# Decode attention with a gated MLP on one core: a PV product with 32 weight columns and 512 moving columns, its diagonal summed on VectorE, and half of V29 queued ahead of K31

## The chip, the core and the metric

One NeuronCore of a Trainium2 chip runs the whole kernel. TensorE (PE) multiplies matrices out of the on-chip memory SBUF into the accumulators PSUM; a matmul is a weight load (its stationary operand) and a stream of moving columns. VectorE (DVE) and ScalarE (ACT) work element by element, SyncE (SP) issues the transfers, and sixteen DMA engines carry them out. Each engine works through its own instructions in order and waits at semaphores for the others. A DMA transfer is split over the sixteen DMA engines, and it has landed when all sixteen have finished their part.

The metric is the device time of one execution in microseconds (us), the median of some runs.

## What is computed

One decoding step for four sequences (B = 4, one token each, D = 640): attention over a sliding window of W = 2048 cached positions with H = 32 heads of Dh = 192, beside a gated MLP (F = 1536), both on the normalised input, added to it. The caches are bfloat16, and the kernel has to read 100 MB of K and as much of V.

```
xn = layernorm(x)
q = (xn @ wq) as [B, H, 1, Dh]
k, v = the last 2048 positions of k_cache, v_cache      # [B, H, 2048, Dh]
p = softmax(einsum("bhqd,bhkd->bhqk", q, k) * Dh ** -0.5)
o = einsum("bhqk,bhkd->bhqd", p, v)
attn = o as [B, 1, H * Dh] @ wo
mlp = (silu(xn @ w1) * (xn @ w3)) @ w2
out = x + attn + mlp
```

## The kernel before

**Layout.** One partition in 128 stands for one of 32 blocks of positions and one of the four sequences (P = 32 x 4); each block has NJ = 64 positions. A K or V tile of one head is 128 x 64 x 192 in bfloat16, 3 MB, and is one transfer. K has two buffers, V three. At the start the V buffers hold wq.

**One head.** The work of a head is cut into GQ = 4 quarters of 16 positions, called units (u = 4 h + quarter; NU = 128 in all):

- `mult` (L227, VectorE): product of a quarter of K with the head's q, 128 x 3072.
- `adder` (L238, TensorE): six matmuls with the identity as weights add groups of 32 of the 192 products in PSUM.
- `reduce_quarter` (L246, VectorE): sums the remaining 32, which gives the scores `sc`.
- `chain_lmax`, `chain_tr`, `chain_gmax`, `chain_bc`, `chain_z` (L250 to L282): maximum over all partitions of a sequence, exponential (`ex`), row sums (`rsum`), and `z`: the exponentials spread over four columns, of which only the own sequence's is not zero.
- `pv` (L290, TensorE): 32 matmuls per head, each with the weights of two positions (2 j x 4 b = 8 columns) against the 2 x 192 = 384 columns of V at these positions. Four strips of PSUM partitions (c = jj % 4, each 32 apart) are used in turn. In the result only the blocks where the position of the weight column and that of the moving column agree are wanted. ScalarE copies the bank to `o_sb` (L297).
- `ge_sum` (L315, TensorE, float32): two products with the selecting weights `sel_w`, one for each position of a pair, each over 192 columns read with a step of six, sum the wanted blocks into the head's 32 partitions of `po`. `ge_tot` (L302) puts the softmax's denominators into a last column of `po`.

**Groups of four heads.** `ge_rec` (L308) inverts the denominators, `ge_turn` scales (`og`, L320) and transposes in blocks of 32 (`oT`, L323), and `ge_proj` (L208) multiplies by the group's part of wo into the accumulator `acc`, which also takes the MLP's output (`ffn_out`) and x itself.

**The order.** The program is written out by hand: each piece of work is put into a numbered slot with a phase, and the slots are emitted in order, within one by phase and then by the order of adding. Slot u holds `mult` of unit u, `adder` and `reduce_quarter` of unit u - 1, and pieces of earlier heads. `pv` of head h is put L = 8 slots after the head's first unit, and `ge_sum` one slot later, except for the last three heads, which have slots of their own (`ends`, L373).

**The loads.** All but the first load (x) come from SyncE in the order of the slots. K of head h is issued at slot 4 (h - 1), when the last product on K of head h - 2 has freed its buffer; V of head h two slots after its first unit. The last three V loads are issued late: V29 at slot NU - 7 = 121, one slot after K31, then V30, V31 (in two halves), w2 in three parts, and the last two parts of wo. At the very end stand `ffn_out(0)`, `ge_proj` of the last two groups, and `ffn_out(1)` and `(2)`, then `res` (L437) and the two stores of the result.

Of the kernel before, what the change touches and what calls it, by code (L numbers as in the profile page):

```python
# [18 lines left out]
def kernel(  # L19
# [36 lines left out]
    CT = 32  # L56
    QW = HG * Dh
    RPP = QW // P
    NU = H * GQ
    N0 = D // 2  # L60
    QC = 512
    NQ = H * Dh // QC
    assert D % P == 0 and F % QC == 0 and P % B == 0 and W % (PB * GQ) == 0
    assert JQ * DD == 512 and JQ % 2 == 0 and 2 * Dh <= 512 and 2 * N0 == D and N0 <= 512
    assert (H * Dh) % QC == 0 and NQ % 6 == 0 and QW % P == 0 and Dh == CT * RPP and P == HG * CT and F == HG * CT * FC
    assert 2 * H * Dh <= NJ * Dh and KBUFS == 2 and VBUFS == 3

# [19 lines left out]
    kts, vts, prs, pss, scs, exs, zs = {}, {}, {}, {}, {}, {}, {}  # L87
    wos, o_sbs, rsums, rts, chs, oTs = {}, {}, {}, {}, {}, {}
# [4 lines left out]
                          in_=k_win[:, h].rearrange("b (p j) d -> p b (j d)", p=PB))  # L93
        kts[h] = kt

    def load_v(h, parts=1):
        vt = vpool.tile([P, NJ, Dh], BF16, tag="vt")
        src = v_win[:, h].rearrange("b (p j) d -> p b j d", p=PB)
        n = NJ // parts
        for j in range(0, NJ, n):  # L100
            nc.sync.dma_start(out=vt[:, j:j + n, :].rearrange("q j d -> q (j d)"),
                              in_=src[:, :, j:j + n, :].rearrange("p b j d -> p b (j d)"))
        vts[h] = vt
# [20 lines left out]
    def ffn_load(name, w):  # L124
# [8 lines left out]
    idf = const.tile([P, P], FP32, name="idf")  # L133
# [4 lines left out]
    mask_f = const.tile([P, B], FP32, name="mask_f")  # L138
# [1 line left out]
    mask_b = const.tile([P, B], BF16, name="mask_b")  # L140
    nc.vector.tensor_copy(out=mask_b[:], in_=mask_f[:])

    rows = const.tile([P, 2 * B], FP32, name="rows")
    nc.vector.tensor_reduce(out=rows[:], in_=idf[:].rearrange("q (c k) -> q k c", k=CT)[:, 0:2 * B, :],
                            axis=AX.X, op=ALU.add)
    NREP = CT // B
    tot_w = head.tile([P, NREP, B], FP32, name="tot_w")
    nc.vector.tensor_copy(out=tot_w[:], in_=mask_f[:].unsqueeze(1).to_broadcast([P, NREP, B]))
    sel_w = const.tile([P, 2, NREP, B], FP32, name="sel_w")
    for par in range(2):  # L150
        nc.vector.tensor_copy(out=sel_w[:, par], in_=rows[:, par * B:(par + 1) * B].unsqueeze(1).to_broadcast([P, NREP, B]))
# [45 lines left out]

    o_banks = []
    for i in range(2):
        o_ps = ps_o.tile([P, 2 * Dh], FP32, tag="o_ps", name="o_ps")  # L200
        nc.vector.memset(o_ps[:], 0.0)
        o_banks.append(o_ps)

    acc = ps_acc.tile([P, N0], FP32, name="acc")
# [80 lines left out]

    def pv(h, j0=0, j1=NJ):
        o_ps, z, vt = o_banks[h % 2], zs[h], vts[h]
        for jj in range(j0 // 2, j1 // 2):
            c = jj % 4
            nc.tensor.matmul(o_ps[c * CT:c * CT + 2 * B, :], lhsT=z[:, 2 * jj:2 * jj + 2, :],  # L290
                             rhs=vt[:, 2 * jj:2 * jj + 2, :], start=(jj < 4), stop=(jj >= NJ // 2 - 4))
        if j1 < NJ:
            return
        zs.pop(h)
        vts.pop(h)
        o_sb = small.tile([P, 2 * Dh], FP32, tag="o_sb", bufs=2, name="o_sb")
        nc.scalar.copy(out=o_sb[:], in_=o_ps[:])  # L297
        o_sbs[h] = o_sb

    def ge_tot(h):  # L300
        sl = slice((h % HG) * CT, (h % HG + 1) * CT)
        nc.tensor.matmul(po[sl, Dh:Dh + 1], lhsT=tot_w[:].rearrange("p a b -> p (a b)"), rhs=rsums.pop(h)[:],  # L302
                         start=True, stop=True)
        chs.pop(h)

    def ge_rec(hg):
        rt = small.tile([P, 1], FP32, tag="rt", bufs=2, name="rt")
        nc.vector.reciprocal(out=rt[:], in_=po[:, Dh:Dh + 1])  # L308
        rts[hg] = rt

    def ge_sum(h):
        sl = slice((h % HG) * CT, (h % HG + 1) * CT)
        o_sb = o_sbs.pop(h)
        for par in range(2):
            nc.tensor.matmul(po[sl, 0:Dh], lhsT=sel_w[:, par].rearrange("p a b -> p (a b)"),  # L315
                             rhs=o_sb[:, par * Dh:(par + 1) * Dh].rearrange("p (r i) -> p i r", i=RPP), start=(par == 0), stop=(par == 1))

    def ge_turn(hg):
        og = small.tile([P, RPP, CT], BF16, tag="og", bufs=1, name="og")
        nc.vector.tensor_scalar_mul(out=og[:].rearrange("p i r -> p (i r)"), in0=po[:, 0:Dh],  # L320
                                    scalar1=rts.pop(hg)[:, 0:1])
        oT = small.tile([P, RPP, CT], BF16, tag="oT", bufs=2, name="oT")
        nc.vector.transpose(out=oT[:].rearrange("p i r -> p (i r)"), in_=og[:].rearrange("p i r -> p (i r)"))  # L323
        oTs[hg] = oT

    def ge_proj(hg, i0, i1):
        oT, wo_t = oTs[hg], wos[hg]
        for i in range(i0, i1):
            acc_add(oT[:, i, 0:B], wo_t[:, i * D:(i + 1) * D])


    FW = F // HG
# [38 lines left out]
    ends = {H - 3: (NU - 1, NU + 1), H - 2: (NU + 2, NU + 3), H - 1: (NU + 6, NU + 7)}  # L373
# [53 lines left out]
    add(e, 6, ge_proj, NG - 1, 0, RPP)
    add(e, 7, ffn_out, 1)
# [42 lines left out]
```

## Time and profile before

| | |
|---|---|
| median of 3 runs | 530.11 us (529.55 to 530.77) |
| profiled execution | 530.9 us, of which the span of the profile is 529.0 |
| granted TensorE clock, mean | 0.893 of full speed |
| TensorE busy, matmuls | 359.1 us (68%), 2306 matmuls, 2307 weight loads |
| VectorE busy | 345.5 us (65%), 435 instructions |
| ScalarE busy | 44.3 us (8%) |
| read from HBM | 222.96 MB, 421 GB/s over the span |
| K to landing after its issue, median | 18.8 us |
| V to landing after its issue, median | 26.6 us |

The profile is of one execution. Its times count from the span's start. Engines are named PE, PEld (TensorE's weight loads), DVE, ACT, POOL, SP; L290 is line 290 of the kernel. In a row of a group of instructions stand the line, the engine, the operation, output <- inputs with shapes, the count, and behind the bars the busy time and the mean duration in ns, and then the time the engine sat idle before them and for whom. In a row of a stretch stand its limits and length, the busy time and the count of each engine, the granted clock, the DMA engines' mean busy share and their GB/s; over a short stretch the share can pass 1, since packets overlap a little and are counted where they begin. The chain that ended last is followed back from the last instruction, at each step to what released it.

### The profile page before, as it was taken

The numbers are of one execution on the slowest core, as the hardware profiler recorded it, in microseconds if no ns is written. First come the engines' busy times: TensorE is split into PE (matmuls) and PEld (weight loads), VectorE is DVE, ScalarE is ACT, GpSimd is POOL, SyncE is SP. The second block draws the span as 40 slices with busy tenths as digits, with TensorE's granted clock in tenths as the row PEclk, the third lists the DMA queues.
The fourth block names the chain that finished last, engine by engine and source line by source line (L and its number), as shares of the span: only waits on it lengthen the run. The fifth ranks groups of instructions, "written<-read, shape, count | busy, mean of one in ns | idle before, by whom it ended". The sixth has DMA issues, their size and how long they took to land.

```text
span 529.0 us, 5427 instructions
## 1 busy us (share of the span) xinstructions
PE 359.1 (68%) x2306; PEld 142.9 (27%) x2307; DVE 345.5 (65%) x435; ACT 44.3 (8%) x142; POOL 1.1 (0%) x8
## 2 busy tenths in 40 slices
PE   2766774768647686587657776776557776766665
PEld 0322221323212222233223322232223232222232
DVE  3179674776837766776746777577647877577920
ACT  2121000000000000000000000000000000000010
POOL 0000000000000000000000000000000000000000
PEclk9989888997959979888888988789987899889997
DMA  8999999999999999999999999999999999999994
GB/s 357 442 421 439 424 429 439 434 429 423 442 427 435 429 431 431 431 431 434 431 427 433 436 418 442 431 431 432 431 436 426 436 426 438 433 429 396 431 403 192
DMA packets 11719, 223.31 MB, mean 422 GB/s; under 512 B 1312, under 2 KB 1456, under 8 KB 2608
## 3 DMA queue, kind: packets, MB, share of 16 engines
q1 hardware_dynamic: 11680, 222.97, 98.4%
q8 instruction: 18, 0.29, 0.2%
q14 instruction: 5, 0.04, 0.0%
q10 hardware_dynamic: 16, 0.01, 0.0%
HBM read 222.96 MB, written 0.01 MB: 421 GB/s over the span
## 4 chain that ended last, share of the span: by engine, by line
DMA 65%; DVE 21%; PE 11%; ACT 1%; issue 1%; SPq 0%
DMA kt<-in_A_k_cache_dram 55%; DVE pr L227 14%; PE ps L238 7%; DMA w<-in_B_w_dram 6%; DMA wt<-in_A_wq_dram 4%; DVE sc L246 3%; PE po L315 3%; PE qps L187 1%; DVE z L282 1%; ACT ex L274 1%; DVE oT L323 1%; PE mt L268 0%; DVE og L320 0%; DVE qbc L193 0%; PE mt L255 0%
## 5 line engine op out<-in xcount | busy, mean ns | idle before, releaser
L238 PE MATMUL ps<-pr,idb 128*128 128x512 bf16 x768 | 215.0, 422 | 143.8 <-DVE pr L227 143.8
L227 DVE TENSOR_TENSOR pr<-kt,qbc 128x3072 bf16<-128x3072 bf16 x128 | 223.4, 1746 | 107.8 <-DMA kt<-in_A_k_cache_dram 107.8
L238 PEld LDWEIGHTS <-idb 128*128 128x128 bf16 x768 | 75.4, 103 | 252.0 <-issue 195.8
L246 DVE TENSOR_REDUCE sc<-ps 128x16 f32<-128x512 f32 x128 | 87.1, 680 | 2.4 <-PE ps L238 2.4
L290 PE MATMUL o_ps<-vt,z 128*8 128x384 bf16 x1024 | 56.2, 358 | 6.0 <-DMA vt<-in_A_v_cache_dram 6.0
L315 PE MATMUL po<-o_sb,sel_w 128*32 128x192 f32 x128 | 49.2, 518 | 1.1 <-ACT o_sb L297 1.1
L290 PEld LDWEIGHTS <-z 128*8 128x8 bf16 x1024 | 25.4, 91 | 36.0 <-issue 25.3
L297 ACT COPY o_sb<-o_ps 128x384 f32<-128x384 f32 x32 | 15.3, 478 | 195.4 <-PE o_ps L290 195.4
L282 DVE TENSOR_TENSOR z<-ex,mask_b 128x256 bf16<-128x256 bf16 x32 | 13.5, 423 | 22.8 <-ACT ex L274 22.8
L271 ACT COPY negm<-mt 128x1 f32<-128x1 f32 x32 | 5.1, 159 | 239.8 <-PE mt L268 239.8
L315 PEld LDWEIGHTS po<-o_sb,sel_w 128*32 128x32 f32 x128 | 13.7, 129 | 28.9 <-issue 26.9
L187 PE MATMUL qps<-wt,xnT 128*128 128x512 bf16 x59 | 16.1, 429 | 5.3 <-DMA wt<-in_A_wq_dram 5.2
L193 DVE CAST qbc<-qps 128x512 bf16<-128x512 f32 x6 | 3.8, 684 | 18.2 <-PE qps L187 18.2
L260 DVE TENSOR_REDUCE gmax<-mt 1x4 f32<-1x128 f32 x32 | 8.8, 275 | 6.8 <-PE mt L255 6.7
L268 PEld LDWEIGHTS mt<-ones_ff,gneg 1*128 1x128 f32 x64 | 9.4, 182 | 13.8 <-issue 12.1
L268 PE MATMUL mt<-ones_ff,gneg 1*128 1x1 f32 x64 | 12.1, 256 | 0.0
L255 PE MATMUL mt<-idf,lmax 128*1 128x128 f32 x32 | 11.1, 348 | 1.1 <-DVE lmax L250 1.1
L274 ACT ACTIVATE ex<-sc,negm 128x64 bf16<-128x64 f32 x32 | 11.1, 348 | 1.0
L187 PEld LDWEIGHTS <-xnT 128*128 128x128 bf16 x60 | 6.4, 107 | 14.6 <-issue 8.7
L208 PE MATMUL acc<-wo_t,oT 128*4 128x320 bf16 x96 | 9.2, 298 | 1.3 <-DMA wo_t<-in_A_wo_dram 1.3
L320 DVE TENSOR_SCALAR og<-po,rt 128x192 bf16<-128x192 f32 x8 | 3.2, 404 | 8.3 <-PE po L315 8.3
L302 PEld LDWEIGHTS po<-rsum,tot_w 128*32 128x32 f32 x64 | 4.5, 108 | 13.3 <-issue 12.7
(52 smaller groups left out, 67.5 us busy)
## 6 DMA issues: line engine op xcount, KB each, us to landing
kt<-in_A_k_cache_dram SPq DMA_DIRECT2D x32, 3072.0 KB, 18.8
vt<-in_A_v_cache_dram SPq DMA_DIRECT2D x31, 3072.0 KB, 26.6
wo_t<-in_A_wo_dram SPq DMA_DIRECT2D x8, 960.0 KB, 20.5
wt<-in_A_wq_dram SPq DMA_DIRECT2D x2, 3072.0 KB, 13.3
w<-in_B_w_dram SPq DMA_DIRECT2D x2, 1920.0 KB, 30.7
vt<-in_A_v_cache_dram SPq DMA_DIRECT2D x2, 1536.0 KB, 32.6
wt<-in_A_wq_dram SPq DMA_DIRECT2D x1, 1536.0 KB
w<-in_B_w_dram SPq DMA_DIRECT2D x1, 1280.0 KB, 35.1
```

The source lines that it names most:

```text
L187: nc.tensor.matmul(qp[:], lhsT=xnT[:, kc].rearrange("p a b -> p (a b)"), rhs=wq_rows[kc][:, (c0 + i) * QC:(c0 + i + 1) * QC], start=(kc == ...
L208: nc.tensor.matmul(acc[i * CT:i * CT + B, :], lhsT=lhsT, rhs=rhs[:, i * N0:(i + 1) * N0], start=first, stop=last)
L227: nc.vector.tensor_tensor(out=pr[:], in0=kts[h][:, g * JQ:(g + 1) * JQ, :], in1=qbc[:, h * Dh:(h + 1) * Dh].unsqueeze(1).to_broadcast([P, ...
L238: nc.tensor.matmul(ps[:], lhsT=idb[:], rhs=pr[:, :, kk * DD:(kk + 1) * DD], start=(kk == 0), stop=(kk == NK - 1))
L246: nc.vector.tensor_reduce(out=scs[h][:, g * JQ:(g + 1) * JQ], in_=pss.pop(u)[:], axis=AX.X, op=ALU.add)
L255: nc.tensor.transpose(out=mt[0:1, 0:P], in_=chs[h][0][:], identity=idf[:])
L268: nc.tensor.matmul(mt[:, P:P + 1], lhsT=gneg[:].rearrange("o p b -> o (p b)"), rhs=ones_ff[0:1, 0:1], start=True, stop=True)
L274: nc.scalar.activation(out=ex[:], in_=scs.pop(h)[:], func=ACTF.Exp, bias=negm[:, 0:1], scale=SCALE, accum_out=rsum[:])
L282: nc.vector.tensor_tensor(out=z[:], in0=ex[:].unsqueeze(2).to_broadcast([P, NJ, B]), in1=mask_b[:].unsqueeze(1).to_broadcast([P, NJ, B]), ...
L290: nc.tensor.matmul(o_ps[c * CT:c * CT + 2 * B, :], lhsT=z[:, 2 * jj:2 * jj + 2, :], rhs=vt[:, 2 * jj:2 * jj + 2, :], start=(jj < 4), stop= ...
L297: nc.scalar.copy(out=o_sb[:], in_=o_ps[:])
L315: nc.tensor.matmul(po[sl, 0:Dh], lhsT=sel_w[:, par].rearrange("p a b -> p (a b)"), rhs=o_sb[:, par * Dh:(par + 1) * Dh].rearrange("p (r i) ...
```

## The change

- `pv` takes eight positions at once: JG = CT // B = 8 positions x 4 sequences = 32 weight columns. The moving operand is 512 columns: eight positions, and of each position's 192 elements (32 groups of RPP = 6) the two elements s * NI and s * NI + 1 of each group, so 64. Three such matmuls (s = 0 to NS - 1 = 2) cover the 192, each into its own strip of 32 partitions. A head takes 8 x 3 = 24 matmuls with as many weight loads, where it took 32.
- `pv_diag` is new, in place of ScalarE's copy: VectorE multiplies the bank (96 partitions x 512) by `jmask`, which keeps in each partition only the columns of its own position, into `o_m`, and sums over the eight positions into `o_sb` (96 x 64). It stands one slot after `pv`, and `ge_sum` a slot later.
- `ge_sum` is one product (weights 96 x 32, 64 columns) instead of two of 192; `og` and `oT` have 64 columns instead of 192; `ge_proj` takes its six pieces from other places of `oT`.
- The two clearings of the PSUM banks at the start go; the constants `jmask`, `smask` and another `sel_w` take the place of `rows` and the old `sel_w`.
- `load_v` takes a range of positions. V29 is loaded in two halves, the first at slot u0 + 2 = 118, ahead of K31, and the second where the whole was.
- The slots of the last three heads move: `pv` of head 29 from 127 to 125, and its `ge_sum` from 129 to 127; `ge_sum` of head 30 from 131 to 132. `ge_proj` of the groups comes one slot later. At the end `ffn_out(0)` is emitted ahead of the last row sums instead of after them.

```diff
-    def load_v(h, parts=1):
-        vt = vpool.tile([P, NJ, Dh], BF16, tag="vt")
+    def load_v(h, j0=0, j1=NJ):
+        if j0 == 0:
+            vts[h] = vpool.tile([P, NJ, Dh], BF16, tag="vt", name="vt")
         src = v_win[:, h].rearrange("b (p j) d -> p b j d", p=PB)
...
+        nc.sync.dma_start(out=vts[h][:, j0:j1, :].rearrange("q j d -> q (j d)"),
+                          in_=src[:, :, j0:j1, :].rearrange("p b j d -> p b (j d)"))
...
-        o_ps = ps_o.tile([P, 2 * Dh], FP32, tag="o_ps", name="o_ps")
-        nc.vector.memset(o_ps[:], 0.0)
+        o_ps = ps_o.tile([P, JG, SW], FP32, tag="o_ps", name="o_ps")
...
-        for jj in range(j0 // 2, j1 // 2):
-            c = jj % 4
-            nc.tensor.matmul(o_ps[c * CT:c * CT + 2 * B, :], lhsT=z[:, 2 * jj:2 * jj + 2, :],
-                             rhs=vt[:, 2 * jj:2 * jj + 2, :], start=(jj < 4), stop=(jj >= NJ // 2 - 4))
...
-        o_sb = small.tile([P, 2 * Dh], FP32, tag="o_sb", bufs=2, name="o_sb")
-        nc.scalar.copy(out=o_sb[:], in_=o_ps[:])
+        for j in range(j0, j1, JG):
+            v = vt[:, j:j + JG, :].rearrange("p j (r i) -> p j r i", i=RPP)
+            for s in range(NS):
+                nc.tensor.matmul(o_ps[s * CT:(s + 1) * CT].rearrange("p j c -> p (j c)"), lhsT=z[:, j:j + JG, :].rearrange("p j b -> p (j b)"),
+                                 rhs=v[:, :, :, s * NI:(s + 1) * NI], start=(j == 0), stop=(j == NJ - JG))
...
+    def pv_diag(h):
+        o_m = small.tile([SR, JG, SW], FP32, tag="o_m", bufs=1, name="o_m")
+        nc.vector.tensor_tensor(out=o_m[:], in0=o_banks[h % 2][0:SR], in1=jmask[0:SR].unsqueeze(2).to_broadcast([SR, JG, SW]),
+                                op=ALU.mult)
+        o_sb = small.tile([SR, SW], FP32, tag="o_sb", bufs=2, name="o_sb")
+        nc.vector.tensor_reduce(out=o_sb[:], in_=o_m[:].rearrange("p j c -> p c j"), axis=AX.X, op=ALU.add)
         o_sbs[h] = o_sb
...
-        for par in range(2):
-            nc.tensor.matmul(po[sl, 0:Dh], lhsT=sel_w[:, par].rearrange("p a b -> p (a b)"),
-                             rhs=o_sb[:, par * Dh:(par + 1) * Dh].rearrange("p (r i) -> p i r", i=RPP), start=(par == 0), stop=(par == 1))
+        nc.tensor.matmul(po[sl, 0:SW], lhsT=sel_w[0:SR].rearrange("p a b -> p (a b)"), rhs=o_sbs.pop(h)[:], start=True, stop=True)
...
-    ends = {H - 3: (NU - 1, NU + 1), H - 2: (NU + 2, NU + 3), H - 1: (NU + 6, NU + 7)}
+    ends = {H - 3: (NU - 3, NU - 2, NU - 1), H - 2: (NU + 2, NU + 3, NU + 4), H - 1: (NU + 6, NU + 7, NU + 7)}
...
-        if h < H - 2:
-            add(u0 + 2 if h < H - 3 else NU - 7, 0, load_v, h)
+        if h < H - 3:
+            add(u0 + 2, 0, load_v, h)
+        elif h == H - 3:
+            add(u0 + 2, 0, load_v, h, 0, NJ // 2)
+            add(NU - 7, 0, load_v, h, NJ // 2, NJ)
...
-        add(m, 7, ge_sum, h)
+        add(d, 8, pv_diag, h)
+        add(m, 8, ge_sum, h)
...
-    add(e - 1, 8, ffn_out, 0)
+    add(e - 1, 7, ffn_out, 0)
     add(e - 1, 8, ge_proj, NG - 2, 0, RPP)
```

More of the change, by code (lines that the diff above doesn't have):

```diff
@@ L61 @@
     QC = 512
+    NI = 2
+    NS = RPP // NI
+    JG = CT // B
+    SW = CT * NI
+    SR = NS * CT
     NQ = H * Dh // QC
     assert D % P == 0 and F % QC == 0 and P % B == 0 and W % (PB * GQ) == 0
-    assert JQ * DD == 512 and JQ % 2 == 0 and 2 * Dh <= 512 and 2 * N0 == D and N0 <= 512
+    assert JQ * DD == 512 and JG * SW == 512 and NS * NI == RPP and NS <= HG and NJ % (2 * JG) == 0 and 2 * N0 == D and N0 <= 512
     assert (H * Dh) % QC == 0 and NQ % 6 == 0 and QW % P == 0 and Dh == CT * RPP and P == HG * CT and F == HG * CT * FC
@@ L94, in load_k @@
         kts[h] = kt
-    def load_v(h, parts=1):
-        vt = vpool.tile([P, NJ, Dh], BF16, tag="vt")
+    def load_v(h, j0=0, j1=NJ):
+        if j0 == 0:
+            vts[h] = vpool.tile([P, NJ, Dh], BF16, tag="vt", name="vt")
         src = v_win[:, h].rearrange("b (p j) d -> p b j d", p=PB)
[L99 to L103, printed above, removed]
+        nc.sync.dma_start(out=vts[h][:, j0:j1, :].rearrange("q j d -> q (j d)"),
+                          in_=src[:, :, j0:j1, :].rearrange("p b j d -> p b (j d)"))
     def wo_load(hg):
@@ L141 @@
     nc.vector.tensor_copy(out=mask_b[:], in_=mask_f[:])
-    rows = const.tile([P, 2 * B], FP32, name="rows")
-    nc.vector.tensor_reduce(out=rows[:], in_=idf[:].rearrange("q (c k) -> q k c", k=CT)[:, 0:2 * B, :],
-                            axis=AX.X, op=ALU.add)
     NREP = CT // B
+    jmask = const.tile([P, NREP], FP32, name="jmask")
+    nc.vector.tensor_reduce(out=jmask[:], in_=idf[:].rearrange("q (s j b) -> q j s b", s=HG, b=B), axis=AX.XY, op=ALU.add)
+    smask = const.tile([P, HG], FP32, name="smask")
+    nc.vector.tensor_reduce(out=smask[:], in_=idf[:].rearrange("q (s k) -> q s k", k=CT), axis=AX.X, op=ALU.add)
     tot_w = head.tile([P, NREP, B], FP32, name="tot_w")
     nc.vector.tensor_copy(out=tot_w[:], in_=mask_f[:].unsqueeze(1).to_broadcast([P, NREP, B]))
-    sel_w = const.tile([P, 2, NREP, B], FP32, name="sel_w")
-    for par in range(2):
-        nc.vector.tensor_copy(out=sel_w[:, par], in_=rows[:, par * B:(par + 1) * B].unsqueeze(1).to_broadcast([P, NREP, B]))
+    sel_w = const.tile([P, NREP, B], FP32, name="sel_w")
+    nc.vector.memset(sel_w[:], 0.0)
+    nc.vector.tensor_tensor(out=sel_w[:, 0:NS], in0=smask[:, 0:NS].unsqueeze(2).to_broadcast([P, NS, B]),
+                            in1=mask_f[:].unsqueeze(1).to_broadcast([P, NS, B]), op=ALU.mult)
     xf = ppool.tile([B, D], FP32, tag="pr")
@@ L212, in acc_add @@
             acc_half(i, lhsT, rhs, last=last)
-    po = ps_po.tile([P, Dh + 1], FP32, name="po")
+    po = ps_po.tile([P, SW + 1], FP32, name="po")
     xr = {}
@@ L287, in pv @@
         o_ps, z, vt = o_banks[h % 2], zs[h], vts[h]
-        for jj in range(j0 // 2, j1 // 2):
-            c = jj % 4
-            nc.tensor.matmul(o_ps[c * CT:c * CT + 2 * B, :], lhsT=z[:, 2 * jj:2 * jj + 2, :],
-                             rhs=vt[:, 2 * jj:2 * jj + 2, :], start=(jj < 4), stop=(jj >= NJ // 2 - 4))
[L292 to L295, printed above, removed]
-        o_sb = small.tile([P, 2 * Dh], FP32, tag="o_sb", bufs=2, name="o_sb")
-        nc.scalar.copy(out=o_sb[:], in_=o_ps[:])
+        for j in range(j0, j1, JG):
[3 more added lines that the diff above has]
+                                 rhs=v[:, :, :, s * NI:(s + 1) * NI], start=(j == 0), stop=(j == NJ - JG))
+        if j1 == NJ:
+            zs.pop(h)
+            vts.pop(h)
+    def pv_diag(h):
[4 more added lines that the diff above has]
+        nc.vector.tensor_reduce(out=o_sb[:], in_=o_m[:].rearrange("p j c -> p c j"), axis=AX.X, op=ALU.add)
         o_sbs[h] = o_sb
@@ L301, in ge_tot @@
         sl = slice((h % HG) * CT, (h % HG + 1) * CT)
-        nc.tensor.matmul(po[sl, Dh:Dh + 1], lhsT=tot_w[:].rearrange("p a b -> p (a b)"), rhs=rsums.pop(h)[:],
+        nc.tensor.matmul(po[sl, SW:SW + 1], lhsT=tot_w[:].rearrange("p a b -> p (a b)"), rhs=rsums.pop(h)[:],
                          start=True, stop=True)
@@ L307, in ge_rec @@
         rt = small.tile([P, 1], FP32, tag="rt", bufs=2, name="rt")
-        nc.vector.reciprocal(out=rt[:], in_=po[:, Dh:Dh + 1])
+        nc.vector.reciprocal(out=rt[:], in_=po[:, SW:SW + 1])
         rts[hg] = rt
@@ L312, in ge_sum @@
         sl = slice((h % HG) * CT, (h % HG + 1) * CT)
-        o_sb = o_sbs.pop(h)
-        for par in range(2):
-            nc.tensor.matmul(po[sl, 0:Dh], lhsT=sel_w[:, par].rearrange("p a b -> p (a b)"),
-                             rhs=o_sb[:, par * Dh:(par + 1) * Dh].rearrange("p (r i) -> p i r", i=RPP), start=(par == 0), stop=(par == 1))
+        nc.tensor.matmul(po[sl, 0:SW], lhsT=sel_w[0:SR].rearrange("p a b -> p (a b)"), rhs=o_sbs.pop(h)[:], start=True, stop=True)
     def ge_turn(hg):
[L319 to L322, printed above, removed]
+        og = small.tile([P, NI, CT], BF16, tag="og", bufs=1, name="og")
+        nc.vector.tensor_scalar_mul(out=og[:], in0=po[:, 0:SW].rearrange("p (r i) -> p i r", i=NI), scalar1=rts.pop(hg)[:, 0:1])
+        oT = small.tile([P, NI, CT], BF16, tag="oT", bufs=2, name="oT")
         nc.vector.transpose(out=oT[:].rearrange("p i r -> p (i r)"), in_=og[:].rearrange("p i r -> p (i r)"))
@@ L328, in ge_proj @@
         for i in range(i0, i1):
-            acc_add(oT[:, i, 0:B], wo_t[:, i * D:(i + 1) * D])
+            acc_add(oT[:, i % NI, i // NI * B:(i // NI + 1) * B], wo_t[:, i * D:(i + 1) * D])
     FW = F // HG
@@ L391 @@
             add(ul + 4, 9, ge_rec, h // HG)
-        v, m = ends.get(h, (u0 + L, u0 + L + 1))
+        v, d, m = ends.get(h, (u0 + L, u0 + L + 1, u0 + L + 2))
         if h < H - 1:
@@ L397 @@
             add(v, 7, pv, h, NJ // 2, NJ)
-        add(m, 7, ge_sum, h)
+        add(d, 8, pv_diag, h)
+        add(m, 8, ge_sum, h)
         if h % HG == HG - 1:
             add(m + 1, 0, ge_turn, h // HG)
-    e = ends[H - 1][1] + 1
+    e = ends[H - 1][2] + 1
     for hg in range(NG - 2):
-        a = ((hg + 1) * HG - 1) * GQ + L + 3
+        a = ((hg + 1) * HG - 1) * GQ + L + 4
         add(hg * HG * GQ + 8, 0, wo_load, hg)
@@ L415 @@
     add(17, 6, x_add, 1)
-    for h in range(H - 2, H):
-        add(NU - 6, 0, load_v, h, 1 + (h == H - 1))
+    add(NU - 6, 0, load_v, H - 2)
+    add(NU - 6, 0, load_v, H - 1, 0, NJ // 2)
+    add(NU - 6, 0, load_v, H - 1, NJ // 2, NJ)
     add(NU - 6, 0, w2_load, 0)
```

## The prediction

> **What bounds the kernel now.** I read the page from the top: how busy the DMA engines are in each slice, what the queues carried, the chain that ended last; then the run cut into stretches; then SyncE's issues and the costliest groups. First the DMA rows of the page:
>
> ```profile
> DMA  8999999999999999999999999999999999999994
> GB/s 357 442 421 439 424 429 439 434 429 423 442 427 435 429 431 431 431 431 434 431 427 433 436 418 442 431 431 432 431 436 426 436 426 438 433 429 396 431 403 192
> ...
> q1 hardware_dynamic: 11680, 222.97, 98.4%
> q8 instruction: 18, 0.29, 0.2%
> ```
>
> The DMA engines are busy in every slice but the first and the last, so every byte counts and nothing that a compute engine saves in the middle can be seen. Next the same, as stretches (the last two columns are the DMA share and GB/s):
>
> ```profile
> 33.00:480.00 447.00, 310.98 (x1981) 122.43 (x1982) 310.98 (x377) 32.56 (x117) 0.00 (x0) 0.88 1.00 431
> 480.00:481.50 1.50, 1.24 (x6) 0.48 (x5) 0.81 (x2) 0.00 (x0) 0.00 (x0) 1.00 0.61 262
> 481.50:504.00 22.50, 15.53 (x122) 7.09 (x120) 19.86 (x24) 1.68 (x7) 0.00 (x0) 1.00 1.01 426
> 504.00:510.00 6.00, 4.87 (x49) 2.13 (x46) 2.20 (x6) 1.08 (x4) 0.00 (x0) 1.00 0.96 373
> ...
> 522.50:523.50 1.00, 0.32 (x6) 0.09 (x1) 0.00 (x0) 0.00 (x0) 0.00 (x0) 1.00 0.13 52
> 523.50:525.50 2.00, 1.22 (x16) 0.70 (x17) 0.00 (x0) 0.00 (x0) 0.00 (x0) 1.00 0.05 20
> ```
>
> Two places stand out. At 480 us the share falls to 0.61. At the end it is 0.13 and then 0.05: 0.13 x 16 is two engines, 0.05 x 16 is one. So the kernel ends with one DMA engine still working, and that engine's queue, not the mean, sets the end. The chain says the same: the last transfer holds it to 525.21, and only 3.8 us follow (span 529.0).
>
> ```profile
> 480.24 12.30 DMA kt<-in_A_k_cache_dram
> 492.54 0.02 issue
> 492.56 32.65 DMA w<-in_B_w_dram
> 525.21 0.04 issue
> 525.26 0.73 PE acc L208 x8
> 525.99 0.02 issue
> 526.01 0.48 DVE res L437
> ```
>
> Why is one engine late? The packet records of the trace give each engine's steps. A packet of 24,576 bytes takes 0.912 us, and a 3 MB load is 8 of them on each engine, 7.27 us. Nothing separates the engines except the instruction loads (queue q8): 18 packets of 16,384 bytes, which go in turn to the same eight engines and each put their engine back by 1.42 us (its completion moves from 0.40 to 1.82 us behind the first engine at 48 us, and the other hits alike). The first sixteen give each of the eight two hits; five smaller ones (8,192 bytes, q14) do about the same to a ninth. So at 480 us seven engines finish K30 at 479.9 to 480.5 and nine at 482.6 to 483.3. K31 is issued at 480.24: the seven have nothing to do until 481.6 to 482.4 (the dip). One of the nine also pauses: it ends K30 at 483.01, starts K31 only at 484.15 with a packet of 1.73 us, and is 1.95 us later from then on. The same engine takes the 17th instruction load at 500.4 (third hit) and ends at 525.36. The engine of the 18th (520.1) ends at 523.42. All others end by 522.32.
>
> SyncE's issues, with their starts, show why K31 comes so late behind K30:
>
> ```profile
> 449.73 0.54 SPq L92 DMA_DIRECT2D kt<-in_A_k_cache_dram  x1
> 450.35 0.56 SPq L101 DMA_DIRECT2D vt<-in_A_v_cache_dram  x1
> 465.26 15.51 SPq L92 DMA_DIRECT2D kt<-in_A_k_cache_dram  x2
> 480.87 3.49 SPq L101 DMA_DIRECT2D vt<-in_A_v_cache_dram  x4
> ```
>
> K29 and V28 go out together, then K30 alone (465.26) and K31 (480.24, after VectorE's last product on K29): no V lies between.
>
> **The change part by part.** *Half of V29 ahead of K31.* V29's buffer is free, so it is issued right after K30 and gives each engine 3.64 us of work (half of 7.27). The seven then run to 483.6, the nine to 486.2 and later. K31's issue moves by what VectorE gains in work per head (1.3 us, below), to 481.5; its first packet can follow 1.3 us after the issue (480.24 to 481.55 now), at 482.8, before 483.6. The dip goes, but only seven early engines gain by that, and they don't end the kernel. What counts is the pause of 1.95 us: it happened to an engine whose next work had been queued 2.8 us before; with 3.64 us more I take it as gone (bounds 0 and 1.95). K31 lands on the slowest engine at 483.33 + 3.64 + 7.27 = 494.2. Its first product began at 494.19, VectorE being busy until then, and now begins 1.3 us later, so this costs nothing; without that cover it would cost VectorE up to 3.6. SyncE's later issues move one place: now L359's last two waits end when the DMA eight issues earlier lands (492.56 K31, about 499.6 V29), with one more issue they end at K31 and V29's second half (494.2, 497.9), some 20 us ahead of their turn. V29 is complete at 497.9; its products now stand two slots earlier, where the sum of products of that slot ran at 498.5. Two transfers become halves: the first half of V31 took 4.02 us on the first engine (504.20 to 508.22), the second 3.75, against 3.64. So 0.1 to 0.4 each, 0.2 to 0.8 for V29's two; I take 0.4.
>
> *PV, row sums, and so TensorE's program.* L290 goes from 1024 matmuls with as many weight loads to 768 of each; L315 from 128 records of each to 64 (32 float32 products, two records each, as now). TensorE's 2306 + 2307 become 4613 - 512 - 128 = 3973. 18 packets for 4613 make 15.5 for 3973: no engine gets a third hit. That is the second part of the gain, 1.42 us on the last engine; if the two packets stay, 0. VectorE's program grows by 65 rows and ScalarE's shrinks by 31, at most one 8,192-byte packet (0 to 0.6 us on the ninth engine; taken 0).
>
> *The cost on the compute engines,* by these groups (mean ns is the second number behind the bar):
>
> ```profile
> L246 DVE TENSOR_REDUCE sc<-ps 128x16 f32<-128x512 f32 x128 | 87.1, 680 | 2.4 <-PE ps L238 2.4
> L290 PE MATMUL o_ps<-vt,z 128*8 128x384 bf16 x1024 | 56.2, 358 | 6.0 <-DMA vt<-in_A_v_cache_dram 6.0
> L315 PE MATMUL po<-o_sb,sel_w 128*32 128x192 f32 x128 | 49.2, 518 | 1.1 <-ACT o_sb L297 1.1
> L297 ACT COPY o_sb<-o_ps 128x384 f32<-128x384 f32 x32 | 15.3, 478 | 195.4 <-PE o_ps L290 195.4
> ```
>
> PV: 32 matmuls of 384 columns took 1.47 us (481.65), 46 ns each, where L238's 512 columns take 243 ns one by one, so 182 for 384: four strips run side by side. Three strips of 512 columns then cost 24 x 243 / 3 = 1.95 us; take 2.0. Upper bounds: one by one 5.8; or the stride of the moving operand slows it as it may slow L315 (365 ns for 192 columns at a step of 24 bytes, 1.9 ns each): 512 x 1.9 x 24 / 3 = 7.8. L290 is the nearer row. The Trainium skill ("TensorE: Matmul & The Clock Gate", Part 3) speaks a little against the change: three column tiles gave 2.38 times, not 3, which would make it an estimated 2.4 us. On the stride, "SBUF — State Buffer" (Door 1, the cacheline note) holds up to 8 bf16 to be free; the new step is two neighbours in every six elements, so by it there is no loss, while L315's 24 bytes would be beyond it.
>
> Row sums: 1.46 us for four records of 192 columns become two records of 64: between 0.38 (two records of one column, L268) and 0.49 (a third); 0.4. ScalarE loses 0.48 per head, none of it on the path but for the last head. VectorE gains two passes over 512 float32 per head, each like L246: 2 x 0.6 to 0.68, so 1.3. The second reads with a step of 256 bytes; L139's strided reduction took 375 ns for 128, and L347, strided, 1824 ns for 384: upper bound 0.68 + 2.4 = 3.1.
>
> In the middle VectorE goes from 10.6 to 11.9 us per head of the 14.6 that the loads take, and K is issued 1.3 us later with 7 us to spare (K29's issue at 449.73, the earliest engine busy until 458.1): nothing. Two memsets of 0.38 at 31 us go, and some 0.4 us of setup comes before xnT, which has 1.7 us until wq lands (8.9 to 10.65): nothing, as the DMA share is full from there on.
>
> At the end, the chain of head 31: z was ready at 509.84, two more pairs of passes lie before it, 512.4. V31 is there by 513.1 (its second half on all engines but the late one), PV ends near 515.3, the passes 516.7; TensorE does L208's first eight chunks meanwhile, as soon as w2 lands (516.1), to 518.4, then the row sums, og and oT (0.9), at 519.8. wo's last load lands near 520.9. So this chain stays about 1 us inside, and the last load still ends the kernel.
>
> **The sum.** 525.36 becomes 522.32 + 0.4 = 522.7: 2.65 us less. On the profiled run's 530.9 that is 528.25. The runs shown have a median of 530.11, 0.8 lower; if all of that carried over, 527.45. I say 528.0.
>
> **Rivals.** *The late engine stays in part* (a pause elsewhere, or a third hit after all, or 0.8 for the halves): it ends at 523.4 + 0.4 to 0.8, so 529.0 to 529.4. For: the pause's cause is not in the profile. Against: the count of 15.5. Chance 0.22, about a third of it under 529.05. *Hidden anyway:* the dip only concerned engines with time to spare, the pause stays with every engine order, 530.1. Chance 0.06. *Slower: PV runs one by one.* 5.8 instead of 1.5 us puts 4.3 into the slots of heads 28 and 29 each while TensorE has 22.5 - 15.5 = 7 us free there; z31 comes at 512.4 + 2 to 8, say 517; PV 5.8, passes 1.4, row sums, og and oT 1.3, products 1.7: 527.2 instead of 525.97, 532.1. It decides as soon as that chain passes 523.4, that is, with PV above some 4.5 us, or with VectorE's two passes above 2.7. Against: L290's 46 ns. Chance 0.12.
>
> **Chances.** Forecast 0.60. What can be told from no change is 0.2%, 1.06 us. Faster: 0.60 + 0.08 = 0.68; within: 0.14 + 0.06 = 0.20; slower 0.12. The range: below, 530.11 - 3.04 = 527.1, a little less with the spread of the runs (0.6), 526.7; above it takes in the second and third case, 530.3; outside is the slower case and little else.
>
> **What would show it.** q8 with 15 or 16 packets. No dip between K30 and K31. The DMA share falling from full to nothing within 1.5 us, near 522.7, and no single engine after it. L290 at 768 with 24 in about 2 us; the two passes at about 0.65 each. I am wrong if the last wait is for oT or VectorE rather than for w2 or wo, or if 0.06 of share runs on past 524.

## The result, and the profile after

The changed kernel takes 532.04 us (median of 15 runs, 529.38 to 533.81). Beside it on the same chip the kernel before took 529.71 us (15 runs, 529.05 to 530.77). The ratio is 1.0044 with a 95% interval of 1.003 to 1.0057: slower by 0.44%, 2.3 us. The forecast was 528.0 and faster, the range ended at 530.3. The profiled execution of the changed kernel took 533.66 us, span 531.9, at the long end of its own runs. These spread over 4.4 us, those of before over 1.7.

The part of the forecast that was about transfers came true. The page of the changed kernel:

```profile
DMA  8999999999999999999999999999999999999991
...
q8 instruction: 15, 0.25, 0.2%
```

Fifteen instruction packets instead of 18, and a last slice that is nearly empty where it had stood at 4. The stretches of the same execution (length, then PE, PEld, DVE, ACT, POOL, granted clock, DMA share, GB/s):

```profile
480.00:481.50 1.50, 0.35 (x2) 0.19 (x2) 1.50 (x2) 0.00 (x0) 0.00 (x0) 1.00 0.99 426
...
495.00:500.00 5.00, 4.79 (x12) 1.70 (x12) 4.42 (x6) 0.00 (x0) 0.00 (x0) 0.50 1.02 440
...
510.00:515.00 5.00, 2.90 (x9) 0.94 (x8) 2.30 (x6) 0.00 (x0) 0.00 (x0) 0.59 1.00 423
515.00:521.00 6.00, 4.09 (x33) 1.55 (x35) 2.19 (x4) 0.60 (x3) 0.00 (x0) 0.50 0.81 335
...
521.50:522.50 1.00, 1.00 (x12) 0.67 (x9) 0.00 (x0) 0.00 (x0) 0.00 (x0) 0.50 0.04 13
522.50:523.50 1.00, 1.00 (x11) 0.65 (x8) 0.00 (x0) 0.00 (x0) 0.00 (x0) 0.50 0.00 0
```

At 480 us the share is 0.99, where it was 0.61: the dip is gone, since half of V29 now goes out between K30 and K31 (SyncE's issues):

```profile
465.79 0.54 SPq L97 DMA_DIRECT2D kt<-in_A_k_cache_dram  x1
466.42 0.56 SPq L105 DMA_DIRECT2D vt<-in_A_v_cache_dram  x1
481.12 0.53 SPq L97 DMA_DIRECT2D kt<-in_A_k_cache_dram  x1
```

Back to the stretches. From 522.5 on there is no transfer at all. The packet records of the loads end at 521.63 or before on fifteen engines and at 521.95 on the last, where one had run to 525.36. (The forecasts of the experiments below take 521.5 to 521.7 for this end.) But the span is longer by 2.9 us, so about 10 us of it now pass without a load. The granted clock (third number from the end) says something more: it is at 0.50 in 495 to 500, and at or near it from 510 to past 523. Before, it was at 1.00 from 495 to 510 and fell only later:

```profile
510.00:515.00 5.00, 2.55 (x27) 0.89 (x22) 0.17 (x1) 0.48 (x1) 0.00 (x0) 0.99 0.99 423
515.00:521.00 6.00, 3.98 (x32) 1.60 (x33) 0.80 (x2) 0.48 (x1) 0.00 (x0) 0.50 1.00 418
```

The chain that ended last, from head 31's last product to the end (start, duration, what):

```profile
508.63 1.68 DVE pr L231
...
510.35 2.26 PE ps L242 x6
...
512.63 0.70 DVE sc L250
...
514.72 0.58 PE mt L272 x2
515.30 1.84 PE o_ps L295 x13
...
517.35 1.55 PE o_ps L295 x9
518.90 0.68 DVE o_m L303
...
519.60 1.01 DVE o_sb L306
...
520.74 0.32 PE po L322
521.06 3.53 PE o_ps L295 x22
...
524.61 0.70 DVE o_m L303
...
525.34 1.02 DVE o_sb L306
...
526.40 0.24 PE po L322
526.64 2.26 PE acc L212 x31
```

Before, this chain held two loads from 480 to 525.21. Now its last load is K30, which lands at 483.90; from there TensorE and VectorE take turns to the end. Read it from 515.30: PV of head 30, the two passes on its result, its row sums (L322, 520.74), and only then PV of head 31 (521.06), its two passes, its row sums, the last products. The timeline shows what PV of head 31 waited for; the bracket gives the engine's idle time before and what ended it:

```profile
516.01 0.42 DVE L286 TENSOR_TENSOR z<-ex,mask_b 128x256 bf16<-128x256 bf16 x1 [1.34 <-ACT ex L278]
...
520.74 0.32 PE L322 MATMUL po<-o_sb,sel_w 96*32 96x64 f32 x1 [1.91 <-DVE rt L317]
...
520.75 0.61 PE L295 MATMUL o_ps<-vt,z 128*32 128x512 bf16 x2
```

Its weights z were ready at 516.43 (516.01 + 0.42), and no wait for V31 is among its rows. TensorE works in order, and ahead of PV31 stood the row sums of head 30, which need VectorE's passes on PV30. So PV31 began 4.3 us after its weights were ready. For some 2.4 us of these TensorE was still at PV30. For the last 1.9 us (the idle time in the bracket) it waited for an instruction that nothing needed before the very end.

The groups (mean ns is the second number behind the bar):

```profile
L295 PE MATMUL o_ps<-vt,z 128*32 128x512 bf16 x768 | 100.1, 531 | 1.4 <-DMA vt<-in_A_v_cache_dram 1.4
...
L306 DVE TENSOR_REDUCE o_sb<-o_m 96x64 f32<-96x512 f32 x32 | 32.4, 1012 | 1.1
L303 DVE TENSOR_TENSOR o_m<-o_ps,jmask 96x512 f32<-96x512 f32 x32 | 21.5, 673 | 6.4 <-PE o_ps L295 6.4
L322 PE MATMUL po<-o_sb,sel_w 96*32 96x64 f32 x64 | 9.7, 234 | 13.2 <-DVE o_sb L306 11.2
```

PV went from 56.2 to 100.1 us of busy TensorE, although it has 768 matmuls instead of 1024. The two passes are 0.67 and 1.01 us each.

### The profile page after: what moved, and what is told of

Read it like the earlier page. It is cut to its first block, busy times and chain, and to the rows that moved or that the text cites. A ratio compares the mean times of both kernels' runs of the same rounds, so it can differ in the third digit from the quotient of the medians.

```text
span 531.9 us, 4826 instructions
## 1 busy us (share of the span) xinstructions
PE 370.4 (70%) x1986; PEld 143.5 (27%) x1987; DVE 392.5 (74%) x498; ACT 29.0 (5%) x110; POOL 1.1 (0%) x8
## 4 chain that ended last, share of the span: by engine, by line
DMA 54%; DVE 34%; PE 10%; issue 1%; ACT 0%; SPq 0%
DMA kt<-in_A_k_cache_dram 50%; DVE pr L231 19%; DVE sc L250 5%; PE ps L242 5%; DMA wt<-in_A_wq_dram 4%; DVE o_sb L306 3%; PE o_ps L295 2%; DVE o_m L303 2%; PE qps L192 1%; DVE z L286 1%; DVE gmax L264 1%; DVE gneg L267 1%; PE acc L212 1%; DVE lmax L254 0%; DVE qbc L198 0%
## 5 line engine op out<-in xcount | busy, mean ns | idle before, releaser
L242 PE MATMUL ps<-pr,idb 128*128 128x512 bf16 x768 | 220.7, 431 | 129.0 <-DVE pr L231 128.7
L242 PEld LDWEIGHTS <-idb 128*128 128x128 bf16 x768 | 78.7, 105 | 240.5 <-issue 182.3
L295 PE MATMUL o_ps<-vt,z 128*32 128x512 bf16 x768 | 100.1, 531 | 1.4 <-DMA vt<-in_A_v_cache_dram 1.4
L295 PEld LDWEIGHTS <-z 128*32 128x32 bf16 x768 | 32.0, 109 | 56.9 <-issue 55.1
L306 DVE TENSOR_REDUCE o_sb<-o_m 96x64 f32<-96x512 f32 x32 | 32.4, 1012 | 1.1
L303 DVE TENSOR_TENSOR o_m<-o_ps,jmask 96x512 f32<-96x512 f32 x32 | 21.5, 673 | 6.4 <-PE o_ps L295 6.4
L322 PE MATMUL po<-o_sb,sel_w 96*32 96x64 f32 x64 | 9.7, 234 | 13.2 <-DVE o_sb L306 11.2
L259 PE MATMUL mt<-idf,lmax 128*1 128x128 f32 x32 | 9.6, 298 | 1.1 <-DVE lmax L254 1.1
L212 PE MATMUL acc<-wo_t,oT 128*4 128x320 bf16 x96 | 9.6, 318 | 0.0
L322 PEld LDWEIGHTS po<-o_sb,sel_w 96*32 96x32 f32 x64 | 4.4, 109 | 17.0 <-DVE o_sb L306 13.8
```

Source lines behind the costliest of these rows:

```text
L212: nc.tensor.matmul(acc[i * CT:i * CT + B, :], lhsT=lhsT, rhs=rhs[:, i * N0:(i + 1) * N0], start=first, stop=last)
L242: nc.tensor.matmul(ps[:], lhsT=idb[:], rhs=pr[:, :, kk * DD:(kk + 1) * DD], start=(kk == 0), stop=(kk == NK - 1))
L295: nc.tensor.matmul(o_ps[s * CT:(s + 1) * CT].rearrange("p j c -> p (j c)"), lhsT=z[:, j:j + JG, :].rearrange("p j b -> p (j b)"), rhs=v[:, ...
L303: nc.vector.tensor_tensor(out=o_m[:], in0=o_banks[h % 2][0:SR], in1=jmask[0:SR].unsqueeze(2).to_broadcast([SR, JG, SW]), op=ALU.mult)
L306: nc.vector.tensor_reduce(out=o_sb[:], in_=o_m[:].rearrange("p j c -> p c j"), axis=AX.X, op=ALU.add)
L322: nc.tensor.matmul(po[sl, 0:SW], lhsT=sel_w[0:SR].rearrange("p a b -> p (a b)"), rhs=o_sbs.pop(h)[:], start=True, stop=True)
```

## The experiments

Three explanations were set against each other: (A) the chain of TensorE and VectorE behind head 31 ends the kernel, with four terms in it: the row sums of head 30 ahead of PV31, a dearer PV, dearer passes, a halved clock; (B) the new order of loads costs time; (C) the half of V29 is a gain that A covers up. Times are medians; the kernel before took 529.47 beside the first four, 529.67 beside the next four, 529.41 beside the last three, and 529.71 beside the change itself, so differences between groups are good to about 0.3 us.

**e1: the row sums of head 30 behind PV31.**

```diff
-    ends = {..., H - 2: (NU + 2, NU + 3, NU + 4), ...}
+    ends = {..., H - 2: (NU + 2, NU + 3, NU + 6), ...}
```

> The changed kernel with the row sums of head 30 moved behind both halves of PV of head 31 on TensorE. Theory A (the end is a chain on TensorE and VectorE; PV of head 31 stands in TensorE's queue behind the row sums of head 30, which wait for VectorE's passes): PV of head 31 starts when PV of head 30 ends (518.9 instead of 520.75), the time falls by some 1.9 us, from 532.0 to about 530.2. Rival B (the new order of the loads is what costs): no change, 532.0.

528.95 us (12 runs, 527.53 to 531.24), ratio 0.9994 (0.9982 to 1.0007): the loss is gone, 3.1 us less than the change, where some 1.9 was expected. PV30 and PV31 run back to back from 513.65 to 519.24, but for a gap of 0.1 us, and a chain of TensorE and VectorE still ends the kernel:

```profile
513.65 1.49 PE o_ps L295 x12
...
515.28 3.96 PE o_ps L295 x29
```

So the wait is real, but it is not the only piece. Its own length in the profile was 1.9 us; what else is in the 3.1 was not taken apart. The clock is a candidate: it was at 1.00 from 511.6 on in e1's profile, and at 0.50 until 524.5 in that of the change.

**e2: V29 whole again, where it stood before.**

```diff
-            add(u0 + 2, 0, load_v, h, 0, NJ // 2)
-            add(NU - 7, 0, load_v, h, NJ // 2, NJ)
+            add(NU - 7, 0, load_v, h)
```

> The changed kernel with V29 loaded whole behind K31, as before. Theory A: the loads do not set the end (all DMA engines were done at 521.5, the kernel ended at 531.9), so the time stays within 1 us of 532.0, though the DMA share dips near 481 us again and K31 lands up to 3.6 us earlier. Rival B: it comes back by 2 us or more, to about 530 or less, and the chain of head 31 begins as much earlier. Either way q8 keeps its 15 packets and no DMA engine works on alone.

532.40 us (11 runs, 529.29 to 533.68), ratio 1.0049 (1.0034 to 1.0065), the same as the change. This excludes B: the old order of loads brings nothing back. The dip at 480 returns (share 0.53), and the DMA engines finish later: fifteen at 522.2 to 522.74, and one works on alone until 523.71, which was not expected. That costs nothing, because the compute chain ends later still.

**e3: the kernel before with the half of V29 alone.**

```diff
...
+        elif h == H - 3:
+            add(u0 + 2, 0, load_v, h, 0, NJ // 2)
+            add(NU - 7, 0, load_v, h, NJ // 2, NJ)
```

> The kernel before with only the two halves of V29, the first ahead of K31. Theory C (the prediction's account of the DMA engines): no dip near 480, no pause of 1.95 us, but still 18 instruction packets and so two engines with a third hit: the last one ends near 523.5 to 524 instead of 525.4, the time falls by 0.5 to 1.8 us, to 528 to 529.2. Rival D (engines and their lateness are not touched by the order): 529.7 unchanged.

528.87 us (11 runs, 528.45 to 529.63), ratio 0.9989 (0.9981 to 0.9998): 0.6 us faster than before. Its stretches and its chain:

```profile
480.00:481.50 1.50, 1.48 (x10) 0.58 (x13) 0.57 (x1) 0.00 (x0) 0.00 (x0) 1.00 0.99 426
...
522.50:523.50 1.00, 0.78 (x14) 0.41 (x9) 0.00 (x0) 0.00 (x0) 0.00 (x0) 1.00 0.05 18
```

```profile
480.00 14.56 DMA kt<-in_A_k_cache_dram
494.57 28.52 DMA w<-in_B_w_dram
```

With 18 instruction packets as before, one engine still ends last (0.05 of 16), but at 523.19 (the next at 522.70) and not at 525.36. C holds: the half of V29 is a gain by itself.

**e4: the moving columns side by side.** Each of the three matmuls takes 64 neighbouring elements of a position instead of two in every six. The columns of the result then stand in another order; the work is the same in number and size.

```diff
-            v = vt[:, j:j + JG, :].rearrange("p j (r i) -> p j r i", i=RPP)
+            v = vt[:, j:j + JG, :]
...
-                                 rhs=v[:, :, :, s * NI:(s + 1) * NI], ...)
+                                 rhs=v[:, :, s * SW:(s + 1) * SW], ...)
```

> The changed kernel with the 64 moving elements of each position taken next to each other instead of two in every six (the columns then belong to other outputs, so the result differs; the work is the same). If the step of the moving operand is what makes a group of three matmuls take 0.34 us instead of 0.215: 24 matmuls take 1.9 to 2.0 us instead of 2.9, and with the end on the compute chain the time falls by 1 to 2 us, to 530 to 531. If it is the weight loads or the number of strips: 2.9 us as now and 532.0.

529.48 us (12 runs, 528.59 to 531.03), ratio 0.9997 (0.9986 to 1.0009), 2.6 us less than the change, where 1 to 2 were expected. One head's PV at full clock, the change first, then e4:

```profile
437.93 2.88 PE L295 MATMUL o_ps<-vt,z 128*32 128x512 bf16 x24
```

```profile
438.15 1.91 PE L295 MATMUL o_ps<-vt,z 128*32 128x512 bf16 x24
```

1.91 us is the forecast's 24 x 243 / 3 = 1.95. The step of the moving operand makes it 2.9. At half the clock the difference is gone; PV30 in the change and in e4, again in this order:

```profile
515.23 2.32 PE L295 MATMUL o_ps<-vt,z 128*32 128x512 bf16 x15
```

```profile
513.05 2.32 PE L295 MATMUL o_ps<-vt,z 128*32 128x512 bf16 x15
```

That would fit a reading of the strided operand which is slower than TensorE at full clock and as quick as it at half; a kernel that reads alone was not run.

**e8: no mask, no sum.** The two passes become one copy of the first 64 columns. The kernel leaves out the masking and the sum over the eight positions.

```diff
-        nc.vector.tensor_tensor(out=o_m[:], in0=o_banks[h % 2][0:SR], in1=jmask[0:SR]..., op=ALU.mult)
...
-        nc.vector.tensor_reduce(out=o_sb[:], in_=o_m[:].rearrange("p j c -> p c j"), axis=AX.X, op=ALU.add)
+        nc.vector.tensor_copy(out=o_sb[:], in_=o_banks[h % 2][0:SR, 0, :])
```

> The changed kernel with VectorE's two passes per head replaced by one copy of 64 columns (it leaves out the mask and the sum over the eight positions). Theory A: each head loses some 1.5 us on VectorE, and four such passes lie before or inside the chain of head 31 (heads 28, 29, 30, 31), so up to 6 us go from the chain and the DMA engines' end (521.6) decides: 526.5 to 528. If TensorE alone makes the chain (PV at 2.9 us and half clock): the passes of heads 30 and 31 give 3 us, and 529.

527.44 us (5 runs, 527.35 to 527.52), ratio 0.9955 (0.9943 to 0.9968). The passes are worth 4.6 us, or more: the chain now ends on a load (`w`, 494.88 to 521.86), which would cover any further gain.

**e9: a warm clock.** 18 matmuls that compute nothing that is used are put into TensorE's waits of the last slots.

```diff
...
+    add(NU, 1, fill, 6)
+    add(NU + 1, 2, fill, 4)
+    add(NU + 2, 2, fill, 2)
+    add(NU + 4, 7, fill, 6)
```

> The changed kernel with 18 more matmuls of 512 columns into a spare PSUM bank, in four places of the last slots at which TensorE waits for VectorE (6, 4, 2 and 6 of them); their result is not used. Theory K (half of the excess, and the spread of the runs, is the granted clock, which was 0.50 to 0.59 between 510 and 525 us): the clock stays near 1 there, PV of heads 30 and 31 takes 2.9 us instead of 3.6, and the time falls to the lower end of the changed kernel's runs, 529.5 to 530.5, with less spread. Otherwise (the extra work only delays what follows): 532 or more.

529.67 us (11 runs, 529.31 to 531.16), ratio 1.0004 (0.9994 to 1.0015), 2.4 us less than the change, and the runs spread over 1.9 us instead of 4.4. Its stretches:

```profile
510.00:515.00 5.00, 4.54 (x36) 1.57 (x34) 1.83 (x5) 0.60 (x3) 0.00 (x0) 1.00 1.00 422
515.00:521.00 6.00, 5.43 (x50) 2.82 (x48) 2.50 (x5) 0.00 (x0) 0.00 (x0) 1.00 0.80 334
```

The clock is 1.00 where it was 0.59 and 0.50. More work on TensorE made the kernel quicker, since the work stands where the engine waited. The profiled execution of e2 shows the same from the other side: it has TensorE's order of the change and no fillers, and it happened to keep its clock,

```profile
515.00:521.00 6.00, 4.09 (x45) 2.21 (x42) 2.53 (x5) 0.00 (x0) 0.00 (x0) 1.00 0.99 416
```

and it took 529.29 us, the lower end of e2's runs and of e9's. It is no full repair: compute still ends it, with span 527.5.

**e5: the mended order.** PV30 goes to slot 127, where TensorE is waiting for VectorE anyway, and its row sums behind PV31.

```diff
-    ends = {..., H - 2: (NU + 2, NU + 3, NU + 4), ...}
+    ends = {..., H - 2: (NU - 1, NU + 3, NU + 6), ...}
```

> The changed kernel with PV of head 30 in slot 127, ahead of the last sums of products, where TensorE waited for VectorE, and the row sums of head 30 behind PV of head 31. Theory A (the end is the chain of head 31 on TensorE and VectorE): PV of head 31 can start as soon as z of head 31 is there, another 2.5 us sooner than with the row sums alone moved (528.95), so the chain comes to the DMA engines' own end (521.6): 526.8 to 527.5, and the last wait is one for w2 or wo. If something else holds the end: 529.

527.36 us (5 runs, 527.25 to 527.49), ratio 0.9954 (0.994 to 0.9968): 4.7 us less than the change and 2.3 less than before, quicker than both. The chain ends on a load again:

```profile
481.11 13.66 DMA kt<-in_A_k_cache_dram
...
494.79 27.04 DMA w<-in_B_w_dram
521.83 0.04 issue
521.88 0.73 PE acc L212 x8
```

It is the end that was forecast, 0.9 us sooner than the 522.7 of the sum.

**e10: e5 with e9's fillers.** Both edits together.

> PV of head 30 in slot 127 and the row sums behind PV of head 31, with the same 18 extra matmuls. If the early PV alone reaches the DMA engines' end: no further gain, 526.8 to 527.5 like it. If the clock still costs there: up to 1 us less than without them, and less spread.

528.40 us (9 runs, 527.99 to 529.44), ratio 0.9975 (0.9965 to 0.9984): 1.0 us worse than e5. Six fillers stand ahead of PV31 in TensorE's order (1.40 us at 514.84), and PV31 begins at 516.24, where it began at 513.77 in e5. A filler is in the queue like any other work.

**e11: e5 with V29 whole.** The edits of e5 and e2 together.

> e5 with V29 loaded whole at slot NU-7, as before the change. In e5 the transfers set the end again (last wait for w, all DMA engines done at 521.7), so what the half of V29 ahead of K31 is worth must show here as it couldn't in e2, where the chain of head 31 covered it. Theory: the empty stretch at 480 us returns and all engines end at 522.2 to 522.7, 0.5 to 1.0 us later; time 527.9 to 528.4, ratio to before 0.9965 to 0.9975. Rival (the half is worth nothing once the chain is mended): 527.4, like e5. Both allow that no single engine is late, since q8 has 15 or 16 packets.

528.86 us (11 runs, 528.54 to 529.33), ratio 0.9987 (0.9978 to 0.9996). The half of V29 is worth 1.4 us where the loads set the end, more than was expected. The stretches and the chain of e11:

```profile
480.00:481.50 1.50, 0.94 (x5) 0.39 (x4) 1.50 (x2) 0.00 (x0) 0.00 (x0) 0.50 0.53 229
...
522.50:523.50 1.00, 0.85 (x14) 0.44 (x10) 0.00 (x0) 0.00 (x0) 0.00 (x0) 1.00 0.29 105
```

```profile
491.41 31.57 DMA w<-in_B_w_dram
```

K31 goes out at 481.28, 1.0 us later than before, since VectorE has more to do per head; so the empty stretch is deeper than it was (0.53 against 0.61), and all sixteen engines end late together, at about 523, with no single one behind.

**e12: of e5's two moves only that of PV30.** The row sums stay ahead of PV31. The edit is shown against e5.

```diff
-    ends = {..., H - 2: (NU - 1, NU + 3, NU + 6), ...}
+    ends = {..., H - 2: (NU - 1, NU + 3, NU + 4), ...}
```

> e5 with the row sums of head 30 left where the change has them (ahead of PV31 in TensorE's order), so of e5's two moves only PV30's. In e5 VectorE had the masked sum of head 30 at 515.4, PV31 began at 513.77. Theory (the row sums are a wait that stands ahead of PV31): PV31 begins only after 515.4, 1.7 us later, and ends near 519; its passes, row sums, og and oT end near 521.7, the products of the last group near 523, res at 523.5, so 0.5 to 1.3 us slower than e5: 527.9 to 528.7, the last wait for oT. Rival (PV30's place is all that counts): 527.4 with the last wait for w.

528.45 us (11 runs, 528.18 to 530.04), ratio 0.9988 (0.9979 to 0.9997). VectorE's z and TensorE in e12:

```profile
513.42 0.42 DVE L286 TENSOR_TENSOR z<-ex,mask_b 128x256 bf16<-128x256 bf16 x1 [1.13 <-ACT ex L278]
...
513.44 0.22 PE L311 MATMUL po<-rsum,tot_w 128*32 128x1 f32 x2 [0.72 <-ACT ex L278]
515.62 0.32 PE L322 MATMUL po<-o_sb,sel_w 96*32 96x64 f32 x1 [1.95 <-DVE rt L317]
```

z of head 31 was ready at 513.84; the row sums hold TensorE for VectorE until 515.62, and PV31 follows them. That puts the end back on the compute chain and costs 1.0 us against e5 on the same chip (below). Both moves are needed.

**e5 again, beside e11 and e12.**

> The same kernel as e5, beside the other two on the same chip, as what they are measured against: 527.2 to 527.6, last wait for w. If it is above 528, the difference between e5 and the change was one of the chip and not of the kernel.

527.41 us (5 runs, 527.33 to 528.2), ratio 0.9965 (0.9953 to 0.9978). Two of the five runs, the profiled one among them, are at 528.2: there the clock was halved from 495 to 500 as in the change (twelve L242 matmuls took 5.27 us), z of head 31 came 1.7 us later than in the first profile of e5, and compute ended it. The mended order has little to spare.

## Why the prediction was wrong

The step that failed is the last of the change's parts: "So this chain stays about 1 us inside, and the last load still ends the kernel." Its own times against those of the profiled run of the change:

| head 31 | forecast | measured | later by, in this step alone |
|---|---|---|---|
| z ready | 512.4 | 516.43 | 4.0 |
| PV begins | 513.1 | 520.75 | 3.6 |
| PV ends | 515.3 | 524.59 | 1.6 |
| the two passes end | 516.7 | 526.36 | 0.4 |
| oT ready | 519.8 | 527.31 | -2.1 |

The last step was shorter than forecast, since L212's first products had run meanwhile. Together 7.5 us. `res` began at 528.92, 5.4 us after the 523.5 at which the forecast's last load and the 0.8 us of products behind it would have let it begin; so the loads had covered some 2.

The first row is the largest, and two things are in it. In e5, where the clock stayed at 1.00 until 514.58, z of head 31 was ready at 513.72. So about 2.7 of the 4.0 us go with the halved clock of the profiled run. The other 1.3 are in part the dearer passes (two pairs stand before z, each 0.4 us above its size in the sum); the rest was not followed up.

- *A wait that the sum didn't have.* The forecast followed VectorE's instructions from z to oT and forgot TensorE's order. It let PV31 begin 0.7 us after z; it began 4.3 us after, since PV30 held TensorE for 2.4 of these and the row sums of head 30 for 1.9. The diff moves these row sums only by one slot, but they now hang on two VectorE passes instead of a ScalarE copy, and stand ahead of PV31. Without the wait the time falls by 3.1 us with PV30 where the change has it (e1), and by 1.0 us with PV30 early (e12 against e5).
- *PV's size.* Taken at 2.0 us, measured 2.9 at full clock and 3.8 for head 31. The number of strips was right (e4: 1.91). The forecast's upper bound for the step of the moving operand, 7.8, was the right place to look, but the value was taken from L290, whose moving columns lie side by side, and which could not show it. The Trainium skill ("SBUF — State Buffer", Door 1, the cacheline note), as the forecast read it, holds a step inside 8 bf16 to be free. e4 disagrees: two neighbours in every six cost 1.0 us of 2.9. On the skill's other figure, that three column tiles give 2.38 times ("TensorE: Matmul & The Clock Gate", Part 3), e4's 1.91 us for 24 x 0.243 us one by one is 3.05 times.
- *The passes.* Taken at 1.3, measured 0.67 + 1.01. The strided reduction was the dearer one, inside the bounds. e8 shows how much hangs on them: each head's pair stands in VectorE's way as well as in the chain.
- *The clock.* All products were counted at full clock. In the profiled run it was halved from 493.8 to 500.6 and from 510.9 to 524.5. e9, which holds it up behind 497, gains 2.4 us.

None of these need have decided alone: taking away any one (e1, e4, e8, e9) brings 2.4 to 4.6 us, which is not additive, as each shortens the same chain until the loads end later. The slower rival had the right place, the chain of head 31 passing the loads' end, and the wrong price: it asked for PV above 4.5 us or passes above 2.7, and the kernel got slower with 2.9 and 1.7. The chance of 0.12 rested on that threshold. That its 532.1 lies so near the measured 532.04 is luck: it was added up from a PV of 5.8 us that runs one by one, and e4 shows that the strips do run side by side.

The steps on the loads were right in direction. The packets came out at 15 (forecast 15.5), the dip went, and the last engine is only 0.3 us behind the next. In e5, where nothing covers them, the last product after the loads begins 3.4 us earlier than in the profile before (521.88 against 525.26). The sizes differ: the halves were to cost 0.4 and "only seven early engines gain" by the dip's filling, but e11 against e5 shows the half to be worth 1.4 us with no late engine in either. With 18 packets (e3) the last engine ends at 523.19, with 15 (the change, e5) at 521.95 and 521.92, so the packets are worth about 1.2 where 1.42 was taken. Whether the pause of 1.95 us in the profile before is a usual thing stays open: with the dip, e2 has one engine that ends 1.0 us behind the next and e11 has none, and the profile before was one of its longer runs.

## What to carry to other kernels

Where a change makes an engine's result later, list what stands behind the instruction that consumes it on the consumer's in-order engine, and not only the chain that the result itself feeds. A price per matmul holds for the access pattern of the row it came from: two matmuls of one size can differ by half if the moving operand is strided. At a kernel's end, where engines wait for each other, count the products at half the clock as one of the cases, and move work that nobody needs yet behind the work that the end waits for.

## What the runs showed of the hardware

- A moving operand of two bfloat16 in every six made a group of three matmuls of 512 columns take 0.36 us instead of 0.24 at full clock (2.90 and 1.91 us for eight groups). At half clock both took 0.43.
- The clock moved in equal steps. In each of the 13 profiles all its changes lie on a grid of 3.413 us (within 1 ns), and the grid lies at another place of the program in each execution. Cut into these steps, the profiles show what goes with a change. After a step at full clock in which TensorE's matmuls were busy for under 0.4 of the time, the next was halved (180 of 180). After one with over 0.6 it never was (0 of 954), and between these it was in 113 of 412. The full clock came back after all 229 halved steps that were busy for over 0.9, and after none of 61 under 0.75.
- In the changed kernel two such steps were 490.39 to 493.80 (busy 0.43, the longest wait 1.96 us) and 507.46 to 510.87 (0.24); the clock was at 0.50 behind them until 500.63 and until 524.52. In the eight profiles with the half of V29 ahead of K31 and the change's passes, the clock fell where a step ended at 493.3 to 493.8 (e9, e5b, the change), and stayed where it ended at 494.1 to 494.5 (e5, e4, e10, e12, e1). So it was where the grid fell that parted e5's two profiles there, as far as these eight go.
- The Trainium skill ("TensorE: Matmul & The Clock Gate", Part 1) names about 3.4 us as the length of an idle stretch that halves the clock. Here shorter waits between sparse work were enough: of the 275 falls behind 33 us in the 13 profiles, 239 had no wait as long as 3.4 us in, or reaching into, the step before.
